# Key-value sums in the ring of PSUM banks, later query and rounding work, and both scan patterns in one PSUM bank, in a fused attention, expert and feed-forward kernel

## The chip, the cores and the metric

The kernel runs on one core of one Trainium2 chip. The metric is the device time of one execution in microseconds (us), the median of the runs shown.

The names in what follows: TensorE does matmuls and transposes, VectorE, ScalarE and GpSimd work on elements, and SyncE (SP) issues DMAs. They take their instructions in program order, each its own, and wait for one another by semaphores. SBUF is the on-chip memory of 128 partitions. PSUM, into which TensorE writes, is divided into banks of 512 fp32 columns per partition.

## The reference

Three layers in a row: a gated linear attention over 4 batches, 8 heads, 768 positions and 48 channels; a mixture of 8 experts with capacity 384 for 3072 tokens of width 384; and a dense feed-forward layer of width 2048.

```python
def _attn_ref(q, k, v, f_logit):
    f = 1.0 / (1.0 + np.exp(-f_logit))
    state = np.zeros((B, H, D, D))
    for t in range(S):
        state = f[:, :, t, :, None] * state + einsum('bhd,bhe->bhde', k[:, :, t], v[:, :, t])
        y[:, :, t] = einsum('bhd,bhde->bhe', q[:, :, t], state)
...
def _moe_ref(x, w_gate, w1, w2):          # N, D, E, F = 3072, 384, 8, 1024; cap = N // E
    order = np.argsort(-(x @ w_gate).flatten())
    # greedily: a token takes its best expert that has room
    for e in range(E):
        h = np.maximum(x[assigned == e] @ w1[e], 0.0)
        out[assigned == e] = h @ w2[e]
...
def _moe2_ref(x, w_in, w_out):            # d_ff 2048
    h = x @ w_in
    g = h * np.clip(h + 3.0, 0.0, 6.0) / 6.0
    return g @ w_out
```

The two weights of the last layer, w_in (384x2048) and w_out (2048x384), come as 64-bit floats.

## The kernel before

**Stages.** Attention takes about the first 175 us of the execution. Routing (which token goes to which expert) follows to about 200 us, and then the experts and the feed-forward layer, one expert at a time, to the end. The order of the instructions on each engine is that in which the Python code calls them (a schedule written out by hand); a waiting instruction holds back all that stand behind it on its engine.

**Attention by chunks.** 3072 tokens are 24 chunks (j) of 128, two of them a unit (u) of 256; there are 12 units, and 3 units are a batch. The recurrence is turned into matmuls inside a chunk and a state of 48x48 per head that goes from chunk to chunk. For this the queries are multiplied by the product of the decays from the chunk's start (the prefix scan, L97), the keys by the product from their place to the chunk's end divided by the whole (the suffix scan, L105). Each scan runs over 260 columns on VectorE, two heads' pairs (p) and both chunks (c) at once, and h=0 and h=1 name its two halves of the four pairs. `tensor_tensor_scan` goes along the columns, multiplies what it has by the decay and takes the maximum with a second tensor, the pattern. The prefix pattern m0 has a 1 where a chunk starts (the scan starts anew there) and 0 elsewhere. The suffix pattern m1 has the reciprocal of the chunk's whole product at its end. `ends` makes it: it takes the maximum of the prefix scan's last column and the limit PMIN (2^-60) into `pmin` (L100) and the reciprocal of that (L101).

**Banks.** m0, the key-value sums KV (L212 writes them) and the limit share one PSUM bank, pC, held for the whole stage; m1 is a pair of SBUF tiles. The other results of TensorE go through a ring of five banks, pT, or through pA0 and pA1 (the masked score products).

**One step of the loop** (lines 269 to 303) handles chunk j and prepares a later unit in eight slots, four in the step of an odd chunk and four in the next step, of an even one (`tg`, PET for TensorE, OPS for VectorE). In the order of the code: slots 0 and 1; the state matmuls of chunk j (L150, from state St) between score matmuls of chunk j+1 (L144, `ya_mm`); the copy of the scores by ScalarE and the causal mask by GpSimd (L177); the output matmuls (L201); the key-value matmuls (L212, `kv_mm`); a query part; slot 2; a decay or query part; the transpose of the keys (`kt_mm`) with ScalarE's copy kt; slot 3. `kv_mm` puts the state's update into the list `late`, which the next slot works off: VectorE adds the sums to the state (L219), GpSimd multiplies by `pmin` (L220). `logits` (L228) goes through the same list.

**refill** prepares a unit's inputs in parts: f by ScalarE and VectorE (L75 to L77), k by VectorE and ScalarE (L80, L81), q by GpSimd (L84 multiplies the even rows, L85 copies the odd ones). After the last part it issues the load of the next unit's input.

**Side work.** `prep` is a generator that VectorE works off in steps beside the attention. `prep_in` (lines 925 to 938) joins the two 32-bit words of each weight of w_in into an fp32 number, 12 tiles of 128x512 from the buffers pw (two, filled by a DMA each): L920, L922 and L924, one step each. Behind L924 it issues the fetch for the tile after the next (into the buffer now free), and splits the number: ScalarE rounds it to fp32r (wih, L717), GpSimd subtracts (wil, L718). `prep_out` (lines 940 to 957) does the like for w_out, in tiles of 128x384; its rounding (L955) is on ScalarE and its subtraction (L957) on VectorE, one step later. How many steps a slot takes is set by two tables:

```python
        PREP=((2,0,1,0),(0,1,1,0)); END=(1,0)
```

The first four numbers are those of the four slots in the step of an odd chunk, the second those of an even one, and END has the two at the step's end. Within a slot the steps come after the slot's first VectorE operation, and before the rest and the late list. The second half of w_out's 16 groups is left for the routing stage (GAP) and the first expert (O1).

Of the kernel before, what the change touches and what calls it, by code (L numbers as in the profile page):

```python
# [17 lines left out]
def attention(tc, q,k,v,f,wg, x_dram, lg, ident, pmin, ranges, prep, setup, spin):  # L18
    nc=tc.nc
    ctx=ExitStack()  # L20
    with ctx:
# [13 lines left out]
        held=ps.tile([128,512],F32,name="pC"); m0=held[:,:W2]; KV=held[:,W2:W2+NP*D].rearrange("p (a d) -> p a d",a=NP)  # L35
        nc.vector.memset(held[:,:W2],0.0); nc.vector.memset(held[:,W2+NP*D:],PMIN)
        nc.vector.memset(m0.rearrange("p (c t) -> p c t",t=L)[:,:,0:1],1.0)
        least=held[:,W2+NP*D:W2+NP*D+1,None].to_broadcast([128,2,2])
        m1=[]
        for i in range(2):  # L40
            t=cs.tile([128,W2],F32,name=f"m1{i}"); nc.vector.memset(t,0.0); m1.append(t)
# [40 lines left out]
        def queries(u,i,h0=0,h1=H):  # L82
            x=view(u,'q')[:,:,h0:h1]
            if i==0: nc.gpsimd.tensor_tensor(out=home('q',0)[:,h0:h1],in0=x[:,0],in1=ft[:,0,h0:h1],op=OP.mult)  # L84
            else: nc.gpsimd.tensor_scalar(home('q',1)[:,h0:h1],x[:,1],1.0,0.0,op0=OP.mult,op1=OP.add)  # L85
        KH={};QT={};PC={};PX={};SX={}
        V=nc.vector
        def decays(u,pairs):
            pt=ps.tile([128,512],F32,name="pT",bufs=PB).rearrange("p (a c g) -> p a c g",a=NP,c=2)
            for p in pairs: nc.tensor.transpose(pt[:,p].rearrange("p c g -> p (c g)"),perm['f'][:,p].rearrange("p a d -> p (a d)"),ident)  # L90
            for h in sorted({p//2 for p in pairs}):
                ff=FF[h][:,:W2].rearrange("p (a c g) -> p a c g",a=2,c=2)
                nc.scalar.copy(ff[:,:,:,1:],pt[:,2*h:2*h+2])
        def prefix(u,h):
            PX[u,h]=wk.tile([128,2,2,L],F32,name="P",bufs=2)
            x=PX[u,h]
            V.tensor_tensor_scan(x.rearrange("p a c g -> p (a c g)"),FF[h][:,:W2],m0,1.0,op0=OP.mult,op1=OP.max)  # L97
        def ends(u,h):
            PC[u]=pmin[:,u]; c=PC[u][:,2*h:2*h+2]
            V.tensor_tensor(out=c,in0=PX[u,h][:,:,:,G],in1=least,op=OP.max)  # L100
            V.reciprocal(m1[h].rearrange("p (a c g) -> p a c g",a=2,c=2)[:,:,:,G],c)  # L101
        def suffix(u,h):
            SX[u,h]=wk.tile([128,2,2,L],F32,name="S",bufs=2)
            x=SX[u,h].rearrange("p a c g -> p (a c g)")
            V.tensor_tensor_scan(x[:,::-1],FF[h][:,1:W2+1][:,::-1],m1[h][:,::-1],0.0,op0=OP.mult,op1=OP.max)  # L105
# [7 lines left out]
        def scaled(u,nm,h):  # L113
# [4 lines left out]
            x=(SX if nm=='k' else PX)[u,h]  # L118
# [8 lines left out]
        OPS={1:((prefix,0),(ends,0)),2:((prefix,1),(suffix,0)),3:((scaled,'q',0),(ends,1)),4:((scaled,'k',0),(suffix,1)),5:((scaled,'q',1),),7:((scaled,'k',1),)}  # L127
# [77 lines left out]
        def kv_mm(j):  # L205
# [3 lines left out]
            pk=KV  # L209
# [35 lines left out]
        for h in range(2):  # L245
# [9 lines left out]
            warm(WARM[1+h])  # L255
        for nm in 'fqk': load(1,nm)
# [11 lines left out]
        PREP=((2,0,1,0),(0,1,1,0)); END=(1,0)  # L268
        for j in range(-1,NCH+1):
# [20 lines left out]
            if ti==1: refill(tu+1,'q',0)  # L290
            tg(2)
            if ti==0: refill(tu+1,'f',0)
            if ti==1: refill(tu+1,'q',1)
            if j+1<NCH: kt_mm(j+1)
            tg(3)
# [610 lines left out]
def gla_moe_ffn(tc,q,k,v,f_logit,moe_w_gate,moe_w1,moe_w2,moe2_w_in,moe2_w_out,out):  # L906
    nc=tc.nc
    with ExitStack() as ctx:
# [16 lines left out]
        def prep_in(pool):  # L925
# [6 lines left out]
            yield  # L932
            for i in range(12):
                yield
                m=pool.tile([128,512],F32,name="pm",bufs=2); c=slice(i%4*512,i%4*512+512)
                yield from join(m,got[i])
                fetch(i+2)
                split_raw(nc,m,wih[:,i//4,c],wil[:,i//4,c],nc.gpsimd)
        woh={}; wol={}
        def prep_out(pool,wr,g0,g1,ahead,W=DM):  # L940
# [7 lines left out]
            for g in range(g0,g1):  # L948
                yield
                m=pool.tile([128,W],F32,name="pm",bufs=2)[:,:DM]  # L950
                yield from join(m,words[g])
# [3 lines left out]
                nc.scalar.copy(woh[g],m)  # L955
                yield
                nc.vector.tensor_tensor(out=wol[g],in0=m,in1=woh[g].bitcast(F32),op=OP.subtract)  # L957
# [177 lines left out]
```

## Time and profile before

| | |
|---|---|
| median of 3 runs (lowest to highest) | 853.25 us (848.27 to 855.46) |
| the profiled execution | 849.52 us |
| its span in the trace | 847.6 us |
| TensorE busy | 795.2 us (94%) |
| VectorE busy | 556.5 us (66%) |
| ScalarE busy | 358.2 us (42%) |
| GpSimd busy | 144.2 us (17%) |
| mean granted TensorE clock | 0.982 |

The span reaches from the first to the last instruction of the trace, and times within it are counted from its start. Busy is the time in which an engine has an instruction at work; TensorE's matmuls are pipelined, so a busy TensorE is not one at its peak. The shares are means over stages with different limits. The granted clock is the share of TensorE's full clock of 2.4 GHz that it got; 0.5 is its lower level, 1.2 GHz. Line numbers (L97) are those of the kernel before; those of the changed kernel lie a few further on (its L98 is L97 before).

### The profile page before, as it was taken

The page shows a single profiled execution, that of the slowest core. Times are in us where ns is not written, and L with a number is a line of the kernel's source. Part 1 is how long each engine was busy: PE and PEld are TensorE (multiplying, and loading weights), DVE is VectorE, ACT ScalarE, POOL GpSimd, SP SyncE. Part 2 cuts the span into 40 slices and gives each one's busy share as a digit, 9 for nine tenths or more (in the row PEclk, how much of TensorE's full clock was granted, in tenths as well). Part 3 has the DMA queues.
Part 4 walks back from the last instruction along what each step waited for, and adds up shares of the span by engine and source line. Part 5 has one row for each costly group of instructions (what it writes and reads, how often), then busy time and mean ns, then how long its engine had stood idle before and what let it go on. Part 6 is the DMA issues. An engine that isn't in the chain of part 4 may idle for free.

```text
span 847.6 us, 16704 instructions
## 1 busy us (share of the span) xinstructions
PE 795.2 (94%) x6387; PEld 763.4 (90%) x6387; DVE 556.5 (66%) x1541; ACT 358.2 (42%) x732; POOL 144.2 (17%) x228
## 2 busy tenths in 40 slices
PE   7788798888999999999999999999999999999994
PEld 6677687778999899999999999999999999999994
DVE  7879899767679647845975676667766523642431
ACT  4656566415244415422542354155315423641431
POOL 3655755202001100110101101100200020010001
PEclk9989999987999999999999999999999999999998
DMA  9877798155004202311421232222232331321000
GB/s 224 204 203 192 205 255 216 50 193 163 1 1 122 84 17 78 91 50 56 122 81 60 83 111 81 88 87 86 79 99 72 97 94 56 113 84 47 10 1 32
DMA packets 99033, 84.55 MB, mean 100 GB/s; under 512 B 67328, under 2 KB 86912, under 8 KB 98944
## 3 DMA queue, kind: packets, MB, share of 16 engines
q1 hardware_dynamic: 95872, 73.96, 31.2%
q0 software_dynamic: 3072, 9.44, 3.5%
q8 instruction: 52, 0.85, 0.4%
q14 instruction: 37, 0.30, 0.1%
HBM read 73.94 MB, written 9.44 MB: 98 GB/s over the span
## 4 chain that ended last, share of the span: by engine, by line
PE 56%; issue 10%; DVE 8%; ACT 3%; DMA 1%; POOL 1%; POOLq 0%; DVEq 0%; ACTq 0%; SPq 0%
PE pF L721 9%; PE acc L721 9%; PE pF L722 9%; PE pF L723 9%; PE acc L723 9%; PE acc L722 9%; DVE ga L864 2%; DVE hl L867 1%; ACT hh L866 1%; ACT ga L863 1%; DVE w1l L770 1%; PE pF L808 1%; POOL out_dram L898 1%; DMA wst<-in_moe_w_dram 1%; DVE q_ge L499 0%
## 5 line engine op out<-in xcount | busy, mean ns | idle before, releaser
L721 PE MATMUL acc<-wo,hh 128*128 128x384 f32 x384 | 133.6, 348 | 0.0
L864 DVE SCALAR_TENSOR_TENSOR ga<-ga,pF 128x384 f32<-128x384 f32 x128 | 70.7, 553 | 92.5 <-ACT ga L863 92.0
L721 PE MATMUL pF<-xh,wih 128*128 128x384 f32 x384 | 131.0, 341 | 0.0
L722 PE MATMUL pF<-xh,wil 128*128 128x384 f32 x384 | 129.4, 337 | 0.0
L723 PE MATMUL acc<-wo,hh 128*128 128x384 f32 x384 | 129.3, 337 | 0.0
L723 PE MATMUL pF<-xl,wih 128*128 128x384 f32 x384 | 129.3, 337 | 0.0
L722 PE MATMUL acc<-wo,hl 128*128 128x384 f32 x384 | 129.1, 336 | 0.1
L863 ACT ACTIVATE ga<-pF,three 128x384 f32<-128x384 f32 x128 | 74.2, 579 | 96.7 <-PE pF L723 89.7
L866 ACT CAST hh<-ga 128x384 fp32r<-128x384 f32 x128 | 65.8, 514 | 97.4 <-DVE ga L864 92.6
L898 POOL DMA_INDIRECT out_dram<-ga,q_ids x24 | 24.3, 1011 | 395.7 <-ACT ga L896 393.0
L867 DVE TENSOR_TENSOR hl<-ga,hh 128x384 fp32r<-128x384 f32 x128 | 71.1, 556 | 29.7 <-ACT hh L866 27.7
L829 ACT ACTIVATE hh<-pF 128x384 fp32r<-128x384 f32 x64 | 31.5, 492 | 132.1 <-PE pF L723 123.1
L830 DVE SCALAR_TENSOR_TENSOR hl<-pF,hh 128x384 fp32r<-128x384 f32 x64 | 35.5, 555 | 70.8 <-ACT hh L829 70.5
L721 PEld LDWEIGHTS acc<-wo,hh 128*128 128x128 f32 x384 | 72.2, 188 | 1.6 <-ACT ga L863 1.5
L722 PEld LDWEIGHTS acc<-wo,hl 128*128 128x128 f32 x384 | 72.2, 188 | 0.4 <-DVE hl L867 0.4
L722 PEld LDWEIGHTS pF<-xh,wil 128*128 128x128 f32 x384 | 72.2, 188 | 0.0
L721 PEld LDWEIGHTS pF<-xh,wih 128*128 128x128 f32 x384 | 72.2, 188 | 0.0
L723 PEld LDWEIGHTS pF<-xl,wih 128*128 128x128 f32 x384 | 72.1, 188 | 0.0
L723 PEld LDWEIGHTS acc<-wo,hh 128*128 128x128 f32 x384 | 72.0, 188 | 0.0
L721 PE MATMUL pF<-xh,w1h 128*128 128x384 f32 x192 | 67.1, 350 | 0.6 <-ACT xh L799 0.6
L721 PE MATMUL acc<-hh,w2h 128*128 128x384 f32 x192 | 65.9, 343 | 0.0
L722 PE MATMUL pF<-xh,w1l 128*128 128x384 f32 x192 | 65.2, 340 | 0.0
(284 smaller groups left out, 1636.7 us busy)
## 6 DMA issues: line engine op xcount, KB each, us to landing
wst<-in_moe_w_dram SPq DMA_DIRECT2D x58, 192.0 KB, 2.4
wst<-in_moe_w_dram SPq DMA_DIRECT2D x42, 256.0 KB, 2.8
pw<-in_moe_w_in_dram SPq DMA_DIRECT2D x12, 512.0 KB, 4.4
wo<-in_moe_w_out_dram SPq DMA_DIRECT2D x16, 384.0 KB, 5.2
pm<-in_moe_w_out_dram SPq DMA_DIRECT2D x32, 192.0 KB, 2.4
pm<-in_moe_w_in_dram SPq DMA_DIRECT2D x30, 192.0 KB, 2.5
v<-in_v_dram SPq DMA_DIRECT2D x24, 192.0 KB, 4.8
x_dram<-y SPq DMA_DIRECT2D x24, 192.0 KB, 5.0
```

Of the source, the lines that this page charges most:

```text
L721: nc.tensor.matmul(out, ahi, bhi, start=start, stop=False)
L722: nc.tensor.matmul(out, alo, bhi, start=False, stop=False)
L723: nc.tensor.matmul(out, ahi, blo, start=False, stop=stop)
L770: nc.vector.tensor_tensor(out=lo,in0=got[i],in1=hi.bitcast(F32),op=OP.subtract)
L808: nc.tensor.transpose(p[:,h*128:(h+1)*128],s.xg[:,h,d*128:(d+1)*128],s.ident)
L829: nc.scalar.activation(hh,p,AF.Relu)
L830: s.defer(2,lambda: nc.vector.scalar_tensor_tensor(hl,p,0.0,hh.bitcast(F32),op0=OP.max,op1=OP.subtract))
L863: nc.scalar.activation(a,p,AF.Relu,bias=s.three[:,0:1])
L864: late(f,1,lambda: nc.vector.scalar_tensor_tensor(g,a,6.0,p,op0=OP.min,op1=OP.mult))
L866: late(f,1,lambda: nc.scalar.copy(gh,g))
L867: late(f,3,lambda: nc.vector.tensor_tensor(out=gl,in0=g,in1=gh.bitcast(F32),op=OP.subtract))
L898: st=nc.gpsimd.indirect_dma_start(out=s.out,out_offset=bass.IndirectOffsetOnAxis(ap=ids[:,t:t+1],axis=0),in_=o,in_offset=None)
```

## The change

1. m0 gets the limit: at the column ahead of each chunk's start, which is the chunk's last product, the pattern holds PMIN, so that the prefix scan itself takes the maximum there. L100 goes, the reciprocal reads the scan's output, and `pmin` is written by a new small ScalarE copy per unit (`kept`), behind slot 2 in the steps of odd chunks. The scans run over 259 columns instead of 260. P becomes two tiles that stay, one per unit in turn.
2. m1 is one pattern instead of two, in the same PSUM bank as m0, and its reciprocal for h=1 stands in slot 2 behind the suffix scan of h=0.
3. KV goes into the ring pT, which stays at five banks.
4. The parts of q come behind `kt_mm`, and ScalarE copies the odd rows.
5. `prep_in` splits a tile one step later than it joins it; `prep_out` rounds a group in the first step of the next group, and subtracts between that one's first and second join. PREP and END change.

```diff
-        held=ps.tile([128,512],F32,name="pC"); m0=held[:,:W2]; KV=held[:,W2:W2+NP*D].rearrange("p (a d) -> p a d",a=NP)
-        nc.vector.memset(held[:,:W2],0.0); nc.vector.memset(held[:,W2+NP*D:],PMIN)
-        nc.vector.memset(m0.rearrange("p (c t) -> p c t",t=L)[:,:,0:1],1.0)
-        least=held[:,W2+NP*D:W2+NP*D+1,None].to_broadcast([128,2,2])
-        m1=[]
+        held=ps.tile([128,512],F32,name="pC"); m0=held[:,:W2-1]; m1=held[:,512-W2:]
+        nc.vector.memset(held,0.0)
+        for n in range(4):
+            nc.vector.memset(held[:,n*L+G-1:n*L+G],PMIN)
+            if n: nc.vector.memset(held[:,n*L-1:n*L],1.0)
+        PXB=[]
         for i in range(2):
-            t=cs.tile([128,W2],F32,name=f"m1{i}"); nc.vector.memset(t,0.0); m1.append(t)
+            t=cs.tile([128,NP,2,L],F32,name=f"P{i}"); nc.vector.memset(t,1.0); PXB.append(t)
...
-            else: nc.gpsimd.tensor_scalar(home('q',1)[:,h0:h1],x[:,1],1.0,0.0,op0=OP.mult,op1=OP.add)
+            else: nc.scalar.copy(home('q',1)[:,h0:h1],x[:,1])
...
         def prefix(u,h):
-            PX[u,h]=wk.tile([128,2,2,L],F32,name="P",bufs=2)
-            x=PX[u,h]
-            V.tensor_tensor_scan(x.rearrange("p a c g -> p (a c g)"),FF[h][:,:W2],m0,1.0,op0=OP.mult,op1=OP.max)
+            PX[u]=PXB[u%2]
+            V.tensor_tensor_scan(flat(PX[u][:,2*h:2*h+2])[:,1:],FF[h][:,1:W2],m0,1.0,op0=OP.mult,op1=OP.max)
         def ends(u,h):
-            PC[u]=pmin[:,u]; c=PC[u][:,2*h:2*h+2]
-            V.tensor_tensor(out=c,in0=PX[u,h][:,:,:,G],in1=least,op=OP.max)
-            V.reciprocal(m1[h].rearrange("p (a c g) -> p a c g",a=2,c=2)[:,:,:,G],c)
+            V.reciprocal(m1.rearrange("p (a c g) -> p a c g",a=2,c=2)[:,:,:,G],PX[u][:,2*h:2*h+2,:,G])
+        def kept(u):
+            PC[u]=pmin[:,u]
+            nc.scalar.copy(PC[u],PX[u][:,:,:,G])
...
-            V.tensor_tensor_scan(x[:,::-1],FF[h][:,1:W2+1][:,::-1],m1[h][:,::-1],0.0,op0=OP.mult,op1=OP.max)
+            V.tensor_tensor_scan(flat(SX[u,h])[:,1:][:,::-1],FF[h][:,2:W2+1][:,::-1],m1[:,1:][:,::-1],0.0,op0=OP.mult,op1=OP.max)
...
-        OPS={1:((prefix,0),(ends,0)),2:((prefix,1),(suffix,0)),3:((scaled,'q',0),(ends,1)),4:((scaled,'k',0),(suffix,1)),5:((scaled,'q',1),),7:((scaled,'k',1),)}
+        OPS={1:((prefix,0),(ends,0)),2:((prefix,1),(suffix,0),(ends,1)),3:((scaled,'q',0),),4:((scaled,'k',0),(suffix,1)),5:((scaled,'q',1),),7:((scaled,'k',1),)}
...
-            pk=KV
+            pk=ps.tile([128,512],F32,name="pT",bufs=PB)[:,:NP*D].rearrange("p (a d) -> p a d",a=NP)
...
-        PREP=((2,0,1,0),(0,1,1,0)); END=(1,0)
+        PREP=((2,0,1,0),(0,0,2,0)); END=(0,1)
...
             if j>=0: kv_mm(j)
-            if ti==1: refill(tu+1,'q',0)
             tg(2)
+            if ti==0 and tu<NU: kept(tu)
             if ti==0: refill(tu+1,'f',0)
-            if ti==1: refill(tu+1,'q',1)
             if j+1<NCH: kt_mm(j+1)
+            if ti==1:
+                for i in range(2): refill(tu+1,'q',i)
             tg(3)
...
+            split=lambda: None
             for i in range(12):
                 yield
+                split()
                 m=pool.tile([128,512],F32,name="pm",bufs=2); c=slice(i%4*512,i%4*512+512)
                 yield from join(m,got[i])
                 fetch(i+2)
-                split_raw(nc,m,wih[:,i//4,c],wil[:,i//4,c],nc.gpsimd)
+                split=lambda i=i,m=m,c=c: split_raw(nc,m,wih[:,i//4,c],wil[:,i//4,c],nc.gpsimd)
+            yield
+            split()
...
-            for g in range(g0,g1):
+            done=None
+            for g in range(g0,g1+1):
                 yield
-                m=pool.tile([128,W],F32,name="pm",bufs=2)[:,:DM]
-                yield from join(m,words[g])
+                if done: nc.scalar.copy(woh[g-1],done)
+                if g<g1:
+                    m=pool.tile([128,W],F32,name="pm",bufs=2)[:,:DM]
+                    parts=join(m,words[g]); next(parts)
+                yield
+                if done: nc.vector.tensor_tensor(out=wol[g-1],in0=done,in1=woh[g-1].bitcast(F32),op=OP.subtract)
+                if g==g1: return
+                yield
+                next(parts)
+                yield
+                next(parts,None)
                 fetch(g+ahead)
                 w=wr.tile([128,2,DM],F32R,name=f"wo{g}")
                 woh[g],wol[g]=w[:,0],w[:,1]
-                nc.scalar.copy(woh[g],m)
-                yield
-                nc.vector.tensor_tensor(out=wol[g],in0=m,in1=woh[g].bitcast(F32),op=OP.subtract)
+                done=m
```

GpSimd's program in one unit of the attention stage, first before and then in the change. am is the masked score, pmq the query, St the state, wil the subtraction's result; r_ones and r_zero are constants of the routing.

```order
L718 TENSOR_TENSOR wil<-pm,wih 128x512
L177 AFFINE_SELECT am<-am 128x512 x2
L84 TENSOR_TENSOR pmq<-qr,ft 128x8x48
L220 TENSOR_TENSOR St_124<-St_122,pmin 128x4x48
L85 TENSOR_SCALAR pmq<-qr 128x8x48
L390 MEMSET r_ones 128x128
L391 MEMSET r_zero 128x24
L718 TENSOR_TENSOR wil<-pm,wih 128x512
L177 AFFINE_SELECT am<-am 128x512 x2
L220 TENSOR_TENSOR St_122<-St_124,pmin 128x4x48
```

```order
L178 AFFINE_SELECT am<-am 128x512 x2
L221 TENSOR_TENSOR St_129<-St_127,pmin 128x4x48
L721 TENSOR_TENSOR wil<-pm,wih 128x512
L85 TENSOR_TENSOR pmq<-qr,ft 128x8x48
L393 MEMSET r_ones 128x128
L394 MEMSET r_zero 128x24
L721 TENSOR_TENSOR wil<-pm,wih 128x512
L178 AFFINE_SELECT am<-am 128x512 x2
L221 TENSOR_TENSOR St_127<-St_129,pmin 128x4x48
```

In the first half of what is shown (an even chunk), the subtraction wil stood ahead of the masks and the query product between masks and state; in the change both stand behind the state multiply, and the query's copy (L85 before) is gone from this engine. In the second half the order is as it was.

VectorE's program from one state sum to the next and on to the next unit's first scan, before. qt and kh are the scaled queries and keys, S the suffix scan's and P the prefix scan's output, m its pattern, pm and pw the joined tile and its words, lg the logits, pmf and pmk the decays and the keys; scans are printed as SCALAR_TENSOR_TENSOR.

```order
L219 TENSOR_TENSOR St_124<-St_124,pC 128x4x48
L124 TENSOR_TENSOR qt<-pT,P 128x512
L100 TENSOR_TENSOR pmin<-P,pC 128x4
L101 RECIPROCAL m_108<-pmin 128x4
L922 SCALAR_TENSOR_TENSOR pm<-pw,pm 128x512
L124 TENSOR_TENSOR kh_121<-pT,S 128x512
L105 SCALAR_TENSOR_TENSOR S<-ff_128,m_108 128x260
L124 TENSOR_TENSOR qt<-pT,P 128x512
L924 SCALAR_TENSOR_TENSOR pm<-pw,pm 128x512
L228 TENSOR_REDUCE lg<-pT 128x8
L77 TENSOR_TENSOR pmf<-ft 128x8x48
L219 TENSOR_TENSOR St_122<-St_122,pC 128x4x48
```

The same stretch in the change:

```order
L220 TENSOR_TENSOR St_129<-St_129,pT 128x4x48
L125 TENSOR_TENSOR qt<-pT,P_113 128x512
L125 TENSOR_TENSOR kh_126<-pT,S 128x512
L106 SCALAR_TENSOR_TENSOR S<-ff_133,pC 128x259
L125 TENSOR_TENSOR qt<-pT,P_113 128x512
L229 TENSOR_REDUCE lg<-pT 128x8
L78 TENSOR_TENSOR pmf<-ft 128x8x48
L220 TENSOR_TENSOR St_127<-St_127,pT 128x4x48
```

Between the two sums the maximum L100, the reciprocal and the two join steps are gone; the rest stands as it stood.

VectorE's program behind that second sum up to the next unit's first scan, before:

```order
L920 TENSOR_SCALAR pm<-pw 128x512
L124 TENSOR_TENSOR kh_121<-pT,S 128x512
L80 TENSOR_TENSOR pmk<-kr,ft 128x8x48
L922 SCALAR_TENSOR_TENSOR pm<-pw,pm 128x512
L924 SCALAR_TENSOR_TENSOR pm<-pw,pm 128x512
L97 SCALAR_TENSOR_TENSOR P<-ff_126,pC 128x260
```

And in the change:

```order
L927 SCALAR_TENSOR_TENSOR pm<-pw,pm 128x512
L923 TENSOR_SCALAR pm<-pw 128x512
L125 TENSOR_TENSOR kh_126<-pT,S 128x512
L81 TENSOR_TENSOR pmk<-kr,ft 128x8x48
L925 SCALAR_TENSOR_TENSOR pm<-pw,pm 128x512
L927 SCALAR_TENSOR_TENSOR pm<-pw,pm 128x512
L923 TENSOR_SCALAR pm<-pw 128x512
L98 SCALAR_TENSOR_TENSOR P_111<-ff_131,pC 128x259
```

Where three join steps stood, five stand: a tile's last step (L927), all three of another tile, and the first (L923) of a third one, which uses the buffer that the first L927 read.

## Rows read from the trace of the kernel before

**Rows 1.** Windows: start:end, length; busy us per engine; PE clock; DMA share; GB/s.

```profile
27.43:150.92 123.49, 101.58 (x1724) 91.14 (x1721) 108.93 (x223) 76.57 (x166) 73.64 (x116) 0.97 0.83 210
40.23:56.70 16.47, 12.60 (x200) 11.27 (x200) 11.57 (x25) 8.36 (x18) 9.29 (x15) 0.90 0.74 192
87.08:101.47 14.39, 11.12 (x212) 9.92 (x206) 12.49 (x25) 8.36 (x18) 10.84 (x17) 1.00 0.83 211
```

The engines stand in the order PE, PEld (weight loads), DVE (VectorE), ACT (ScalarE), POOL (GpSimd); the number of instructions is in parentheses.

**Rows 2.** Waits of VectorE, 27.43 to 150.92: us in total, times, longest.

```profile
DVE P L97 <- PE pC L212: 8.5, 6, 4.7
DVE qt L124 <- PE pT L111: 2.2, 1, 2.2
DVE wo L957 <- ACT wo L955: 1.2, 2, 0.6
DVE St L219 <- PE pC L212: 0.8, 2, 0.4
DVE St L217 <- PE pC L212: 0.3, 1, 0.3
```

**Rows 3.** Timeline of VectorE: start, us, instruction, [idle before, and its releaser].

```profile
82.01 0.35 DVE L219 TENSOR_TENSOR St<-St,pC 128x192 f32<-128x192 f32 x1 [0.40 <-PE pC L212]
...
84.77 1.48 DVE L922 SCALAR_TENSOR_TENSOR pm<-pw,pm 128x512 uint32<-128x512 uint32 x1
...
89.73 0.70 DVE L97 TENSOR_TENSOR_SCAN P<-ff,pC 128x260 f32<-128x260 f32 x1 [1.32 <-PE pC L212]
...
91.27 0.33 DVE L219 TENSOR_TENSOR St<-St,pC 128x192 f32<-128x192 f32 x1
...
92.40 0.66 DVE L922 SCALAR_TENSOR_TENSOR pm<-pw,pm 128x512 uint32<-128x512 uint32 x1
...
96.41 0.35 DVE L219 TENSOR_TENSOR St<-St,pC 128x192 f32<-128x192 f32 x1 [0.40 <-PE pC L212]
...
101.47 0.68 DVE L97 TENSOR_TENSOR_SCAN P<-ff,pC 128x260 f32<-128x260 f32 x1
```

**Rows 4.** Timeline of GpSimd in the same unit.

```profile
83.01 1.42 POOL L177 TENSOR_SCALAR_AFFINE_SELECT am<-am 128x512 f32<-128x512 f32 x2
84.40 1.29 POOL L84 TENSOR_TENSOR pmq<-qr,ft 128x384 f32<-128x384 f32 x1
85.66 0.95 POOL L220 TENSOR_TENSOR St<-St,pmin 128x192 f32<-128x192 f32 x1
```

**Rows 5.** Timeline of TensorE in two units, from state matmul to key-value matmul.

```profile
41.69 0.48 PE L150 MATMUL pT<-qt,St 64*64 64x128 f32 x2 [3.08 <-POOL St L220]
...
45.60 0.62 PE L212 MATMUL pC<-v,kt 128*64 128x48 f32 x16
...
86.67 0.33 PE L150 MATMUL pT<-qt,St 64*64 64x128 f32 x2 [2.44 <-POOL St L220]
...
89.06 0.62 PE L212 MATMUL pC<-v,kt 128*64 128x48 f32 x16
```

**Rows 6.** Windows, as rows 1, of two microseconds behind the first.

```profile
42.00:44.00 2.00, 2.00 (x44) 2.00 (x40) 0.00 (x0) 0.00 (x0) 1.57 (x4) 0.50 0.72 243
```

**Rows 7.** Groups by form, 30 to 166: times, busy us, mean ns, idle before.

```profile
L105 DVE TENSOR_TENSOR_SCAN S<-ff,m 128x260 f32<-128x260 f32 x20 | 16.8, 839 | 0.0
L97 DVE TENSOR_TENSOR_SCAN P<-ff,pC 128x260 f32<-128x260 f32 x18 | 12.4, 688 | 8.6 <-PE pC L212 8.6
...
L81 ACT COPY pmk<-kr 128x384 f32<-128x384 f32 x9 | 4.9, 540 | 0.0
L100 DVE TENSOR_TENSOR pmin<-P,pC 128x4 f32<-128x4 f32 x19 | 2.9, 154 | 0.3
```

**Rows 8.** DMA issues on the page: times, KB each, median us to landing.

```profile
pw<-in_moe_w_in_dram SPq DMA_DIRECT2D x12, 512.0 KB, 4.4
```

**Rows 9.** Waits of VectorE, 150.92 to 166.

```profile
DVE wo L957 <- ACT wo L955: 2.3, 4, 0.6
DVE P L97 <- PE pC L212: 0.5, 1, 0.5
```

More of the change, by code (lines that the diff above doesn't have):

```diff
@@ L93, in decays @@
                 nc.scalar.copy(ff[:,:,:,1:],pt[:,2*h:2*h+2])
+        flat=lambda t: t.rearrange("p a c g -> p (a c g)")
         def prefix(u,h):
-            PX[u,h]=wk.tile([128,2,2,L],F32,name="P",bufs=2)
-            x=PX[u,h]
-            V.tensor_tensor_scan(x.rearrange("p a c g -> p (a c g)"),FF[h][:,:W2],m0,1.0,op0=OP.mult,op1=OP.max)
+            PX[u]=PXB[u%2]
+            V.tensor_tensor_scan(flat(PX[u][:,2*h:2*h+2])[:,1:],FF[h][:,1:W2],m0,1.0,op0=OP.mult,op1=OP.max)
         def ends(u,h):
-            PC[u]=pmin[:,u]; c=PC[u][:,2*h:2*h+2]
-            V.tensor_tensor(out=c,in0=PX[u,h][:,:,:,G],in1=least,op=OP.max)
-            V.reciprocal(m1[h].rearrange("p (a c g) -> p a c g",a=2,c=2)[:,:,:,G],c)
+            V.reciprocal(m1.rearrange("p (a c g) -> p a c g",a=2,c=2)[:,:,:,G],PX[u][:,2*h:2*h+2,:,G])
+        def kept(u):
+            PC[u]=pmin[:,u]
+            nc.scalar.copy(PC[u],PX[u][:,:,:,G])
         def suffix(u,h):
             SX[u,h]=wk.tile([128,2,2,L],F32,name="S",bufs=2)
-            x=SX[u,h].rearrange("p a c g -> p (a c g)")
-            V.tensor_tensor_scan(x[:,::-1],FF[h][:,1:W2+1][:,::-1],m1[h][:,::-1],0.0,op0=OP.mult,op1=OP.max)
+            V.tensor_tensor_scan(flat(SX[u,h])[:,1:][:,::-1],FF[h][:,2:W2+1][:,::-1],m1[:,1:][:,::-1],0.0,op0=OP.mult,op1=OP.max)
         PT={}
@@ L117, in scaled @@
             pt=PT.pop((u,nm,h))
-            x=(SX if nm=='k' else PX)[u,h]
+            x=SX[u,h] if nm=='k' else PX[u][:,2*h:2*h+2]
             x=x.rearrange("p a c g -> p (a c) g")
@@ L255, in attention @@
             warm(WARM[1+h])
+        kept(0)
         for nm in 'fqk': load(1,nm)
```

## The prediction

> **What bounds the kernel now.** The mean rows by stage come first. From 201 us on TensorE streams matmuls and the change touches little there; the change lies in the attention stage, 0 to about 175 us, so I cut that stage by its own clock, the unit (one h=0 scan L97 to the next). Nine units, 27.43 to 150.92, take 123.49 us, 13.72 each [rows 1]. VectorE is busy 108.93 us of them, TensorE 101.58, ScalarE 76.57, GpSimd 73.64, and the DMA engines at a share of 0.83. So VectorE sets the pace, with 14.56 us of idle time, and TensorE is close behind: a unit can fall only until one of the two, or the state chain that runs through both, is full.
>
> The view of waits says what the idle time is. The second scan of a unit (L97) waits 8.5 us in six places for the key-value matmul L212, up to 4.7 us [rows 2]. That scan reads nothing of L212; both only use bank pC. A query product waits 2.2 us and state sums 0.8 and 0.3 for matmuls of TensorE, and L957 waits 1.2 us in two places, 0.6 each, for the rounding ScalarE has just been given. Together that is 13.0 us.
>
> The timelines of one unit, 87.08 to 101.47, show why L212 is late. The state sum of the chunk before ends on VectorE at 82.36, but GpSimd multiplies it only at 85.66, behind two mask selects (83.01) and the query product L84 (84.40) [rows 3, 4]. TensorE waits 2.44 us for it and starts its state matmuls at 86.67; the key-value matmuls run from 89.06 to 89.68, and the scan starts at 89.73, 1.32 us late [rows 3, 5]. In the unit from 40.23 the same wait was 3.08 us; after it TensorE's granted clock was 0.50, its lower level, and the way from state matmul to key-value matmul took 41.69 to 45.60, 3.9 us where the later unit needs 2.4 [rows 5, 6]. That unit took 16.47 us with VectorE busy 11.57 [rows 1].
>
> **The change part by part**, for the nine units first.
>
> *Limit in the scan.* Two L100 go per unit, at 154 ns [rows 7]: 18 x 0.154 = **-2.8 us**. Their outputs now come from one small ScalarE copy per unit, which waits for the second scan; ScalarE is 62% busy, and I cost it at nothing. If its cover were gone it would hold back the kt copy behind it, and with it the logit matmuls, by a few tenths per unit: it is in the upper bound.
>
> *Suffix scan reads pC instead of m1.* The suffix scan L105 takes 839 ns on average and the prefix scan L97, which reads the bank already, 688 [rows 7]. That work of VectorE on SBUF is stretched beside GpSimd, the join step L922 shows: 1.48 us at 84.77, beside the query product, and 0.66 at 92.40 [rows 3, 4]. I take the whole difference, 18 x 0.151 = **-2.7 us**; bounds 0 (GpSimd's work stretches a neighbour instead) and 2.7. The Trainium skill (SBUF — State Buffer, Who interferes with whom) says that a VectorE instruction with two SBUF inputs contends with a GpSimd instruction that reads SBUF, and one with at most one does not; by that rule the stretch of L105 goes entirely, and the rows agree with it.
>
> *kv in the ring, q and wil behind the state.* The second scan then waits for no matmul, and GpSimd's order puts the state multiply right behind the selects, ahead of wil and L84 (the order rows on GpSimd). In the unit above it could start near 84.4 instead of 85.66, or sooner, since wil no longer stands ahead of the selects; the matmuls of that half move forward by 1.3 to 2.4 us, which ends VectorE's 1.32 us wait and leaves the 4.7 us one no cause. Of the 14.56 us idle I drop the 13.0 of the waits above: 8.5 for L97, 2.2, 0.8 and 0.3 that followed the same late matmuls, 1.2 for L957: **-13.0 us**. The order of work bounds it: 14.56 at most, and little at the least (third rival).
>
> *What is late next: the state chain.* In the order rows on VectorE, L922 and L924 stood between the two state sums of a unit; in the change their like stand outside. The chain from one sum to the next is unchanged: sum at 91.27, state matmul 1.11 us later, and from state matmul to the point where VectorE can go on 89.73 - 86.67 = 3.06 [rows 3, 5]: 4.17 us. The work that VectorE now has in between is 96.01 - 91.27 = 4.74 (to 96.41 less 0.40, where the next sum began to wait) less an L100 (and part of L101), 0.3, less L922 and L924, at about 0.6 each: 3.2 us. So the second sum waits about 0.9 us in each of the six of the nine units that carry the state in both halves: **+5.4 us**; bounds 2.4 (0.40 each, as the wait before the sum at 96.41 is now [rows 3]) and 8.5 (the ring's new kt release adds half a microsecond).
>
> *The pw fetch.* By the order rows, tile B's last join step L927 now stands with five instructions between it and the next use of its buffer (L923). The fetch for that use is issued by the end of L927. Five instructions of the same kinds ran from the sum's end at 96.76 to 101.47, 4.71 us [rows 3]; a fetch lands 4.4 us after issue [rows 8], and for issue and semaphore I allow 0.5. That is 0.2 us late. If GpSimd stretched fewer of the five (L922's 0.66 for its 1.48) they would take some 2 us less. I take 0.5 us in five units: **+2.5 us**, bounds 0 and 10.
>
> *Outside the nine units.* Behind 150.92 go one L97 wait of 0.5 and three of the four L957 waits of 0.6 (the last lies where VectorE no longer sets the pace) [rows 9]: **-2.2 us**, bounds 0.8 and 3.5, the more if the masks no longer queue behind a rounding. In routing L957 stands on the path with such a wait too, and with the roundings a step later that goes and one join step leaves the gap before: **-1.0 us**, by one wait of 0.6 and two thirds of an L922 (0 to 1.3). At the start VectorE sets seven single columns (at most an L100 each, 1.1) and clears two tiles of twice the size (at most an L922 each, 1.3), while the first loads are under way: **+0.5 us**, bounds 0 and 2.4.
>
> *At nothing:* the query copy, now 0.54 us of ScalarE per unit [rows 7] instead of GpSimd work; it stands behind a rounding and the kt copy and ahead of the decay copies that the next h=0 scan needs. That scan comes over 4 us later on VectorE (96.76 to 101.47 [rows 3]), against some 3 us of copies; without that cover it costs 0.5 per unit.
>
> Sum: -2.8 - 2.7 - 13.0 + 5.4 + 2.5 - 2.2 - 1.0 + 0.5 = **-13.3 us**. The profiled execution took 849.52 us, so 836.2; it lies 3.7 below the median of the three runs shown, 853.25, and the same step from there gives 840. I forecast **838 us**. The nine units come to about 113 us, 12.5 each.
>
> **Rivals.** (1) *The clock falls in the new wait.* TensorE will idle about 1.9 us per unit ahead of the second half's state matmuls, for the sum that VectorE reaches late. For it: 3.08 us of idle was followed by 0.50. Against: 2.44 was not (clock 1.00 from 87.08 on) [rows 1, 5, 6]. Price: 3.9 - 2.4 = 1.5 us, on the chain each time, six units: +9, so 847. The Trainium skill (TensorE: Matmul & The Clock Gate, HAM oscillation — how this bites in real kernels) warns that a wait repeated in every turn of a loop can throttle every turn anew; by that rule it would be every unit, and the trace shows it in the longer waits only.
>
> (2) *DMA takes the gain.* The nine units hold 0.83 x 123.49 = 102.5 us of DMA time; in 113 us that is a share of 0.91. If transfers start to wait, and the units stay at 0.85, they take 120.6: +7.7, so 846. Against: of VectorE's waits in these units none is for a transfer [rows 2].
>
> (3) *The change doesn't do what it says.* If the state multiply stays as late (its sum is late on VectorE rather than queued on GpSimd), the wait only moves from the scan to the state sum, and the -13.0 and +5.4 fall away: -5.7, so 844.
>
> (4) *The other side: the pw fetch is late.* Six times in the stage VectorE would stand at L923 with the scan, and so the whole unit, behind it. The gain is gone when each stall is 0.5 + 13.3 / 6 = 2.7 us, at a landing of about 7 us; at 9 us it is 4.7 each, +25 on the sum, so 861. Against: 4.4 us is the landing now, with the queries and keys not yet issued at that moment.
>
> (5) *More than forecast:* neither new wait appears: 828.
>
> **How the numbers follow.** Forecast (831 to 843) 0.53; rival 1 0.08, 2 0.12, 3 0.13, 4 0.07, rival 5 0.07. The forecast's own range is 831 to 843; the range to 8 in 10 reaches down to rival 5 and up past 1 and 2: 828 to 848. About 1% (8.5 us against 853.25, so 844.7) is what a measurement of this kernel can tell from no change. Faster: forecast, rival 5 and most of rival 3, 0.70; same: 1, 2 and the rest of 3, 0.23; slower: 4, 0.07.
>
> **What would show it.** Right: no L97 wait for a matmul; L105's heir at 0.69 in every place; GpSimd's state multiply within 0.1 us of its sum in second halves; waits of 0.4 to 1.4 us before the second sum of a unit; units near 12.5 us and a granted clock of 1.00 throughout. Wrong: clock rows of 0.50 between 40 and 110 (rival 1), VectorE waiting for pw by microseconds (4) or for k (2), the state multiply still microseconds behind its sum (3). The forecast as a whole is wrong if the nine units take over 120 us.

## The result, and the profile after

| | before | changed |
|---|---|---|
| median (lowest to highest) | 853.10 us (848.27 to 855.46) | 843.22 us (839.63 to 845.23) |
| ratio, 95% interval | | 0.9882, 0.9855 to 0.9909 |
| the profiled execution, its span | 849.52, 847.6 us | 845.23, 843.2 us |
| nine units (first scan to first scan) | 123.49 us | 117.97 us |
| VectorE busy, idle in them | 108.93, 14.56 us | 101.42, 16.55 us |
| mean granted clock | 0.982 | 0.982 |

The change made the kernel faster by 9.9 us or 1.2%: the side that was forecast, at two thirds of the size (838 us). The median of 843.22 lies 0.2 us above the forecast's own range (831 to 843) and inside the wide one (828 to 848). The two profiled executions differ by only 4.3 us, since the one of before was among its fastest and the one of after is its slowest; sums over the two traces therefore fall 5.6 us short of the medians.

The windows of after, columns as in [rows 1], give all nine units, a usual one, a long one, and six microseconds within the long one:

```profile
27.78:145.75 117.97, 101.63 (x1724) 91.14 (x1722) 101.42 (x203) 80.58 (x183) 65.97 (x107) 0.97 0.87 220
41.71:55.59 13.88, 11.10 (x188) 9.78 (x188) 12.13 (x24) 9.00 (x22) 9.07 (x14) 1.00 0.84 221
82.60:99.36 16.76, 14.20 (x188) 12.64 (x188) 12.07 (x23) 8.91 (x21) 9.23 (x14) 0.80 0.78 183
86.28:92.28 6.00, 6.00 (x68) 5.49 (x70) 2.72 (x6) 2.39 (x5) 1.89 (x6) 0.50 1.22 249
```

VectorE's work fell by 7.5 us (the maxima L100 are gone, the suffix scans take 12.3 us instead of 15.4, and one join step and one subtraction fewer fall into the stretch), but its idle time did not fall, it rose. What it waits for is another thing now. The view of waits of VectorE over the nine units, which answers to [rows 2]:

```profile
DVE St L220 <- PE pT L213: 9.7, 6, 4.1
DVE pm L923 <- DMA wo<-in_moe_w_out_dram: 2.5, 1, 2.5
DVE pm L923 <- DMA pw<-in_moe_w_in_dram: 2.1, 3, 1.0
DVE lg L229 <- ACT y L232: 0.5, 1, 0.5
```

The second scan waits for nothing any more. Instead the second state sum of a unit (L220, L219 before) waits for the key-value matmul, six times, and the join waits for its words. GpSimd does what it was to do: the state multiply that belongs to the second sum of a unit now follows the masks, ahead of the subtraction and the query product. It starts 0.1 us behind its sum in all six places, where it was 0.6 to 4.8 us behind before, 3.3 us in the unit shown there [rows 3, 4]. One second sum of after on VectorE, then GpSimd:

```profile
76.83 0.35 DVE L220 TENSOR_TENSOR St<-St,pT 128x192 f32<-128x192 f32 x1 [1.12 <-PE pT L213]
```

```profile
75.96 1.22 POOL L178 TENSOR_SCALAR_AFFINE_SELECT am<-am 128x512 f32<-128x512 f32 x2 [2.08 <-ACT am L177]
77.27 0.89 POOL L221 TENSOR_TENSOR St<-St,pmin 128x192 f32<-128x192 f32 x1
78.52 1.28 POOL L721 TENSOR_TENSOR wil<-pm,wih 128x512 fp32r<-128x512 f32 x1 [0.36 <-ACT wih L720]
79.76 1.32 POOL L85 TENSOR_TENSOR pmq<-qr,ft 128x384 f32<-128x384 f32 x1
```

### The profile page after: what moved, and what is told of

Its sections match the earlier page's. It is cut to its first block, busy times and chain, and to the rows that moved or that the text cites. A ratio compares the mean times of both kernels' runs of the same rounds, so it can differ in the third digit from the quotient of the medians.

```text
span 843.2 us, 16692 instructions
## 1 busy us (share of the span) xinstructions
PE 793.5 (94%) x6387; PEld 761.9 (90%) x6387; DVE 549.6 (65%) x1522; ACT 364.0 (43%) x757; POOL 134.7 (16%) x215
## 4 chain that ended last, share of the span: by engine, by line
PE 57%; issue 10%; DVE 8%; ACT 2%; DMA 2%; POOL 1%; POOLq 0%; SPq 0%; DVEq 0%; ACTq 0%
PE pF L724 9%; PE acc L724 9%; PE pF L725 9%; PE pF L726 9%; PE acc L726 9%; PE acc L725 9%; DMA xg<-x_dram,q_ids 1%; DVE ga L867 1%; DVE hl L870 1%; ACT hh L869 1%; DVE w1l L773 1%; PE pF L811 1%; POOL out_dram L901 1%; DVE q_ge L502 1%; POOL xg L790 1%
## 5 line engine op out<-in xcount | busy, mean ns | idle before, releaser
L726 PE MATMUL pF<-xl,w1h 128*128 128x384 f32 x192 | 64.9, 338 | 0.0
```

What stands on the lines that cost most here:

```text
L726: nc.tensor.matmul(out, ahi, blo, start=False, stop=stop)
```

## The experiments

All medians are of executions timed beside the kernel before on the same chip (its median 851.9 us in the first four runs, 852.7 in the next four, 851.1 in the last four).

| run | what it is | median (lowest to highest) | ratio to before, 95% interval |
|---|---|---|---|
| e1 | before, key-value sums in the ring | 847.10 (845.1 to 850.3) | 0.9942 (0.9919 to 0.9965) |
| e2 | changed, key-value sums back | 845.12 (844.13 to 846.62) | 0.9918 (0.9891 to 0.9946) |
| e3 | changed, suffix pattern back in SBUF | 843.24 (841.58 to 845.57) | 0.9905 (0.9875 to 0.9935) |
| e4 | changed, order of side work back | 842.84 (839.00 to 846.34) | 0.9904 (0.9873 to 0.9936) |
| e5 | changed, handling of joined tiles back | 836.94 (835.06 to 838.31) | 0.9820 (0.9792 to 0.9848) |
| i1 | changed, split at the step's end | 843.48 (840.88 to 843.86) | 0.9891 (0.9866 to 0.9915) |
| i2 | changed, three word buffers | 842.01 (840.24 to 842.89) | 0.9877 (0.9853 to 0.9901) |
| i4 | i1 with the old tables | 835.05 (833.72 to 837.26) | 0.9806 (0.9778 to 0.9834) |
| e7 | changed, old tables: two join steps between the sums | 835.95 (834.92 to 836.66) | 0.9821 (0.9796 to 0.9846) |
| e8 | changed, one join step between | 834.43 (833.49 to 838.80) | 0.9814 (0.9785 to 0.9842) |
| e9 | changed, none between, the others spread | 840.48 (836.83 to 842.02) | 0.9864 (0.9839 to 0.9890) |
| i5 | i4 with w_out's first fetches earlier | 835.59 (833.81 to 837.32) | 0.9818 (0.9793 to 0.9843) |

### e1: the ring alone

```diff
-            pk=KV
+            pk=ps.tile([128,512],F32,name="pT",bufs=PB)[:,:NP*D].rearrange("p (a d) -> p a d",a=NP)
```

> The kernel before with one part of the change alone: the key-value sums go into the ring of five banks instead of pC. Theory (the prediction's): the second scan then waits for no matmul, which takes the 9.0 us of its waits away; the state multiply on GpSimd stays behind the query product, so TensorE still waits some 14 us for it, and the sums that VectorE then reaches sooner wait a little longer. Expected 844 to 848 us against 853, second-scan waits 0, waits of the state sums 3 to 5 us in place of 0.8. Rival A (the wait only moves from the scan to the state sum): 850 to 854, with state-sum waits of 8 us or more. Rival B (the ring of five banks gets too small with one user more): 853 or slower, with TensorE waiting for ScalarE's copies out of the ring by 10 us or more.

Measured 847.1, in the theory's range. VectorE's waits show that both it and rival A had a part: no scan waits, but the state sums wait 6.9 us in place of 0.8, near A's 8.

```profile
DVE St L219 <- PE pT L212: 6.9, 6, 3.3
DVE qt L124 <- PE pT L111: 3.3, 3, 1.7
```

So of 9.0 us of scan waits some 5 were gained. Rival B falls: no wait of TensorE for a copy of yt passes 0.8 us.

### e2: the ring undone in the changed kernel

KV goes back to `held[:,W2:W2+NP*D]` and L214 writes there; the suffix pattern goes to SBUF, as in e3.

> The changed kernel with the key-value sums back in bank pC; as they don't fit beside both patterns, the suffix pattern is back in two SBUF tiles. The limit in the scan and the new order stay. Theory: the second scan waits again for the key-value matmul of the step, some 5 to 9 us, and the suffix scans cost 2.7 us more: 849 to 853 against 843 of the change. Rival A (the ring only moves the wait): 844 to 847, the suffix scan's 2.7 alone, with state-sum waits small again. Rival B (the ring is too small in the change): 841 to 844, and TensorE's waits for the copies of yt, 13.7 us in the change, mostly gone.

Measured 845.1, the time of rival A, though not by its reason, as the state sums still wait. With this order the scan comes late, and the shared bank couples the other way: now the matmul waits for the scan more than the scan for the matmul. Waits of VectorE, then of TensorE, over its nine units:

```profile
DVE St L221 <- PE pC L214: 6.3, 6, 1.9
DVE P L99 <- PE pC L214: 3.9, 6, 1.0
```

```profile
PE pC L214 <- DVE P L99: 8.9, 5, 3.7
```

### e3: the suffix pattern in SBUF

```diff
-held=ps.tile([128,512],F32,name="pC"); m0=held[:,:W2-1]; m1=held[:,512-W2:]
+held=ps.tile([128,512],F32,name="pC"); m0=held[:,:W2-1]
...
+            t=cs.tile([128,W2],F32,name=f"m1{i}"); nc.vector.memset(t,0.0); m1.append(t)
```

> The changed kernel with the suffix pattern alone back in two SBUF tiles; the key-value sums stay in the ring. Theory: the suffix scans are stretched beside GpSimd again, mean 0.83 us instead of 0.68 in 20 of them: 845 to 847 against 843. Rival (the stretch only moves to the VectorE instruction beside it, or into waits that are there anyway): 842 to 844, though the suffix scan's mean goes up.

The rival's result: 843.24 against 843.22, though the scan's mean went from 682 to 832 ns. The groups by form over nine units, first of after, then of e3:

```profile
L106 DVE TENSOR_TENSOR_SCAN S<-ff,pC 128x259 f32<-128x259 f32 x18 | 12.3, 682 | 0.0
```

```profile
L107 DVE TENSOR_TENSOR_SCAN S<-ff,m 128x259 f32<-128x259 f32 x18 | 15.0, 832 | 0.0
```

The 2.7 us are there in the scan and not in the time. In after VectorE is busy 101.42 us and idle 16.55 in the nine units, in e3 103.30 and 12.78: what the scan saves became waiting. One of a unit's two suffix scans lies between the state sums, where VectorE waits anyway; that this hides it is argued, no run isolates it.

e2 and e3 differ in the ring alone, 845.12 and 843.24 us. So with the new order the ring is worth 1.9 us by the medians, and the executions of the two overlap, where it gave 4.8 by itself (e1).

### e4: the old order of the side work

The query parts, the split, `prep_out` and the tables are those of before; the ring and both patterns stay.

> The changed kernel with its order of side work undone: the query parts ahead of the transposes and on GpSimd as before, the split of a joined tile right behind the join, the old tables of steps. The ring and the two patterns in one bank stay. Theory: the state multiply stands behind the query product again, so TensorE waits for it again (7 to 14 us in place of 0.2), of which VectorE's state sums show some; the waits for the fetched words (4.6 us) go: 845 to 849 against 843. Rival C (the new order gives nothing, since ScalarE's rounding now stands ahead of the copies of the next step and waits for the join, 19 us, and TensorE waits 13.7 us for the copies of yt behind it): 839 to 844.

Measured 842.84, the same as the change: rival C's time. TensorE waits for the state multiply again, 10.7 us:

```profile
PE pT L151 <- POOL St L221: 10.7, 6, 2.4
```

So the whole new order is worth nothing. Either its parts do nothing or one takes what another gives. Rival C named a taker: ScalarE's rounding. The next four runs take the parts one by one.

### e5, i1, i2 and i4: which part takes it

e5 has `prep_in`, `prep_out` and the tables of before. i2 has `bufs=3` for pw and fetches three tiles ahead. i1 collects the splits in a list and works it off at the end of the loop's step; i4 is i1 with the old tables.

```diff
-                split=lambda i=i,m=m,c=c: split_raw(nc,m,wih[:,i//4,c],wil[:,i//4,c],nc.gpsimd)
+                SPLITS.append(lambda i=i,m=m,c=c: split_raw(nc,m,wih[:,i//4,c],wil[:,i//4,c],nc.gpsimd))
...
+            while SPLITS: SPLITS.pop(0)()
             if j>=0: next(constants,None)
```

> The changed kernel with only its handling of the joined tiles undone (split right behind the join, old tables of steps); q stays late and partly on ScalarE, the ring and the patterns stay. Theory H (in the change ScalarE's rounding, now beside the next tile's first join step, stands ahead of the copies of the next step and waits up to 2.6 us for the join's last step on VectorE; TensorE waits 13.5 us for the copies of yt behind it, and this eats what the late q gives): 837 to 841 against 843, with TensorE's waits for yt below 4 us and those for the state multiply below 8 us. Rival F (it is the late fetches, 4.6 us of VectorE's waits): these go here too, 838 to 841, but TensorE's waits for yt stay. Rival N (neither was on the path, since another chain has the same length): 842 to 845.

> The changed kernel with the split of a joined tile (ScalarE's rounding and GpSimd's subtraction) issued at the end of the loop's step, behind the query and key copies, when the join's last step is long done. Nothing else moves. Theory H: ScalarE's waits for the join, 19.1 us in the change, fall below 6; TensorE's waits for yt fall from 13.5 to below 4; 838 to 841 against 843. Rival F: the late fetches stay (4.6 us), 842 to 844. Rival N: 842 to 845, and the waits turn up elsewhere.

> The changed kernel with three buffers for the fetched words instead of two, each fetch a tile earlier; nothing else moves. Rival F (late fetches are what the change pays with): VectorE's waits for pw, 2.1 us, go, and 840 to 842 against 843. Theory H: the rounding's wait on ScalarE and TensorE's wait for yt stay as they are, and VectorE only waits for its state sums instead: 842 to 844.

> As the run with the split at the end of the loop's step, and with the old tables of steps too, so that two join steps stand between the state sums again and the fetches are spread more evenly. Theory H with F: no wait for pw, none of ScalarE for the join, none of TensorE for the state multiply or yt: 836 to 840. By the prediction's fourth step (the state chain is next once VectorE has less work between the sums) this is 1 to 3 us faster than with the new tables; rival (that chain does not bind): the same within 1 us.

e5 took 836.9 us, 6 less than the change and than e4: the late query is worth that much, and the handling of the joined tiles, tables included, takes it. Theory H (the rounding) falls by i1: TensorE's waits for yt, 13.5 us, fell to 1.6, and the time stayed at 843.5. ScalarE only waits elsewhere; its waits in after, then in i1:

```profile
ACT wih L720 <- DVE pm L927: 19.1, 12, 2.6
```

```profile
ACT pmin L104 <- DVE P L99: 16.0, 7, 4.2
```

Both are waits for VectorE, which is the engine that is late. Rival F (the words) falls as the main cause by i2: no wait for pw is left, and the median is 1.2 us lower, within the uncertainty. i4 differs from i1 in the tables alone and took 835.05 against 843.48 on the same chip; their executions don't overlap. The tables cost 8.4 us (7 by the ratios).

### e7, e8, e9 and i5: what about the tables

```diff
-        PREP=((2,0,1,0),(0,0,2,0)); END=(0,1)
+        PREP=((2,0,1,0),(0,1,1,0)); END=(1,0)
```

```diff
-        PREP=((2,0,1,0),(0,0,2,0)); END=(0,1)
+        PREP=((2,0,1,0),(0,1,2,0)); END=(0,0)
```

```diff
-        PREP=((2,0,1,0),(0,0,2,0)); END=(0,1)
+        PREP=((1,0,3,0),(0,0,2,0)); END=(0,0)
```

These are e7, e8 and e9. Between the second sum of a unit and the first of the next stand six join steps in after and e9, five in e8 and four in e7. i5 draws the start of `prep_out`, with its first three fetches, ahead of the 31st step of `prep_in`.

> The changed kernel with only the two tables of steps back, so that two join steps stand between the two state sums of a unit again (none in the change) and three in a row ahead of the next unit's first scan (five in the change). The split stays a step late. Theory C (the chain from state sum to state sum through TensorE is longer than the work that the new tables leave VectorE between the sums, so VectorE waits and TensorE after it): state-sum waits fall from 12.2 us in eight to under 5; 835 to 838 against 843. Theory P (the five join steps in a row hold up the next unit's scans, and with them TensorE): the same time, since both are undone. Theory H (the split's place is what costs): 841 to 844.

> The changed kernel with tables that put one join step between the two state sums and four ahead of the next first scan, two of them ahead of the keys' product. Theory C: about half the way, 838 to 841; state-sum waits 5 to 9 us. Theory P: 840 to 842, since the pile is one step shorter.

> The changed kernel with tables that leave no join step between the state sums, as the change does, but spread the others: three ahead of the next first scan instead of five, three behind the unit's second scan. Theory C: 842 to 845, state-sum waits of 10 us or more. Theory P: 836 to 839, though no step stands between the sums.

e7, the tables alone undone, took 835.95; e8, with one join step between the sums, 834.43, all of the gain and not half of it; e9, with none between, 840.48. By theory C e9 should have been at 842 or more, by P at 839 or less; it lies between. By the medians most of the price is that of the empty place between the sums. That the pile of five has a share is not shown: the executions of e9 and of the change overlap, and e9 has no wait for fetched words in the nine units, of which after has 4.6 us (two kinds, w_in's and w_out's). e7 beside e5 (835.95 and 836.94, ratios 0.9821 and 0.9820) says one thing more: with the old tables, it makes no difference whether the split stands right behind the join or a step later.

The timelines of VectorE, state sums only, first two units of after, then one unit and the next first sum of e8 and of e7:

```profile
30.82 0.34 DVE L220 TENSOR_TENSOR St<-St,pT 128x192 f32<-128x192 f32 x1
...
35.42 0.36 DVE L220 TENSOR_TENSOR St<-St,pT 128x192 f32<-128x192 f32 x1 [1.32 <-PE pT L213]
...
44.80 0.34 DVE L220 TENSOR_TENSOR St<-St,pT 128x192 f32<-128x192 f32 x1
...
49.07 0.36 DVE L220 TENSOR_TENSOR St<-St,pT 128x192 f32<-128x192 f32 x1 [0.99 <-PE pT L213]
```

```profile
31.15 0.34 DVE L220 TENSOR_TENSOR St<-St,pT 128x192 f32<-128x192 f32 x1
...
35.75 0.35 DVE L220 TENSOR_TENSOR St<-St,pT 128x192 f32<-128x192 f32 x1 [0.72 <-PE pT L213]
...
43.61 0.34 DVE L220 TENSOR_TENSOR St<-St,pT 128x192 f32<-128x192 f32 x1
```

```profile
30.32 0.34 DVE L220 TENSOR_TENSOR St<-St,pT 128x192 f32<-128x192 f32 x1
...
35.06 0.34 DVE L220 TENSOR_TENSOR St<-St,pT 128x192 f32<-128x192 f32 x1
...
43.42 0.34 DVE L220 TENSOR_TENSOR St<-St,pT 128x192 f32<-128x192 f32 x1
```

From the first sum of a unit to the second it takes 4.60 us in after and in e8, where VectorE waits for the second sum, and 4.74 in e7, where it doesn't. So the chain through GpSimd and TensorE sets it in the first two (4.27 to 4.60 us in the full-clock units of after), and one join step there is free. From the second sum to the next first one it takes 9.38, 7.86 and 8.36 us. There VectorE waits for nothing but words (0.43 us in after), so its own work sets the time, but not by the count of steps: e7 has one step fewer there than e8 and takes 0.5 us longer, since its key product and its join steps take longer beside GpSimd. The key products, first e7, then e8:

```profile
36.44 1.50 DVE L81 TENSOR_TENSOR pmk<-kr,ft 128x384 f32<-128x384 f32 x1
```

```profile
37.88 1.03 DVE L81 TENSOR_TENSOR pmk<-kr,ft 128x384 f32<-128x384 f32 x1
```

One unit took 13.88 us in after (41.71 to 55.59) and 12.47 in e8 (40.60 to 53.07):

```profile
40.60:53.07 12.47, 11.72 (x202) 10.18 (x199) 11.65 (x24) 8.64 (x21) 9.04 (x13) 1.00 0.96 242
```

The 1.41 us are 0.27 of the sum's wait (0.99 to 0.72), 0.65 of a wait for pw that e8 hasn't in this unit, and 0.48 of VectorE's busy time (12.13 to 11.65), the join steps and the key product being stretched more in after. Such a wait for pw stands in three of the nine units of after.

The clock seems to have a share too. e9 and e8 differ by 6.1 us over the nine units of their traces, and all of it lies in the two units of e9 in which the granted clock fell; the other seven take 83.6 us in e9 and 83.8 in e8 (which waits 3.1 us for words there). Not all of it need be the clock's, as VectorE is also busy 1.9 us longer in the first of the two. The two units of e9, then the same two of e8:

```profile
27.33:43.75 16.42, 14.14 (x240) 13.00 (x231) 13.50 (x24) 10.25 (x23) 8.99 (x14) 0.90 0.76 188
68.74:83.53 14.79, 12.66 (x196) 11.43 (x198) 11.91 (x24) 9.39 (x22) 8.70 (x14) 0.88 0.85 216
```

```profile
28.15:40.60 12.45, 12.09 (x226) 10.96 (x224) 11.63 (x24) 9.25 (x22) 9.08 (x13) 1.00 1.00 244
66.60:78.97 12.37, 10.60 (x196) 9.71 (x196) 11.55 (x24) 7.40 (x18) 7.12 (x12) 1.00 0.94 236
```

At full clock the four other units with both sums took 49.4 us in e9 and 47.1 in e8, so by these two traces the empty place costs 0.6 us in each, on average. Of the 9.3 us between after and e8, 4.3 lie in the one unit of after whose clock fell; of the 8.0 between i1 and i4, 5.2 lie in two such units of i1.

> The run with the split at the step's end and the old tables, which took 835.05 us, with the first three fetches of w_out's words issued some two tiles earlier. There VectorE waited 3.2 us for the first of them, once. If that wait is on the path: 831 to 833, and no wait of L925 for w_out left. If the wait only stands where VectorE would wait for the state anyway: 834 to 836.

i5 took 835.59, the second case: no wait for w_out was left, but VectorE's busy time in the nine units went from 103.27 to 106.08 us, and one unit had a granted clock of 0.84.

The best of these runs, e8, is 0.9814 of before, 16.7 us; it cannot be told from i4, e7, i5 and e5.

## Why the prediction was right, and where it was off

**The sign was right, the size was 5 us too large, at the upper edge of the range.** The nine units were to take about 113 us and took 117.97. The work of VectorE fell by more than was said (7.5 us for 5.5); the miss is in its idle time, which was to fall by 5.1 us and rose by 2.0. Of these 7.1 us, 4.3 are the waits of the state sums (9.7 for 5.4, above the bound of 8.5) and 2.5 a wait for w_out's words. Step by step:

*The cause, the late state multiply and the shared bank:* right. No scan waits for a matmul, and TensorE's wait for the multiply fell from 13.8 us in seven places to 0.2 in one. The ring alone gave 4.8 us (e1), the late query about 6 (e4 to e5). Together with the other parts, but with the tables left as they were (e7), the gain is 15.2 us, where the prediction's terms without the two new waits come to 21.2. In the nine units of e7 VectorE's idle time fell from 14.56 to 3.73 us, so 10.8 of the 13.0 came; its work fell by 3.5 where 5.5 was said.

```profile
27.63:136.83 109.20, 98.42 (x1708) 87.75 (x1706) 105.47 (x202) 80.19 (x181) 67.25 (x107) 1.00 0.93 234
```

*Suffix pattern in PSUM, -2.7:* the scan does what was said, 682 ns everywhere, in agreement with the rule of the Trainium skill that the prediction named (SBUF — State Buffer, Who interferes with whom). The step that failed is to take the whole difference as a gain: the lower bound, 0, was right. In the change it made no difference (e3). Where VectorE hardly waits, in e7, the suffix scans' 15.4 us became 12.3, but the key product went from a mean of 919 ns to 1236 (2.8 us over nine), and the first join step from 648 to 778. Which part of the change put them beside GpSimd is open: between e3 and after, which differ in the pattern alone, the key product stays at 1020 ns.

*State chain, +5.4, and pw fetch, +2.5:* the mechanism and the place were right. The waits in full-clock units were 1.32, 0.99, 1.12, 0.92 and 1.31 us where 0.9 was said, since the chain took up to 4.60 us and not 4.17; one, in the unit whose clock fell, was 4.07. Undoing the tables, which removes both terms, gave 8.4 us (i4 against i1) where 7.9 was forecast; e7 against the change gives 7.3 by the medians and 5 by the ratios. That the whole comes so near may be luck in part, as these differences also hold the units whose clock fell. What the prediction lacked was the conclusion: it named this as a price and did not ask whether the step could be left out.

*A wait not foreseen:* the first fetch of w_out, 2.5 us, once. That the join had been moved nearer to it is not the whole cause, as e3 has the joins in the same order and no such wait. When it was taken away in i5, the time stayed as it was.

*Outside the units:* behind them the trace shows -1.5 (from 26.28 to 24.82 us up to the first routing step, 177.20 and 170.57), where -2.2 was said. Routing did not fall by 1.0 but took 24.78 us instead of 23.03 to the first expert matmul; TensorE waits 5.7 us there for gathered rows, 1.7 before. In before and the three runs with the old handling of the tiles (e1, e4, e5) this stretch took 22.4 to 23.8 us, in the change and the nine runs with the rounding moved 22.8 to 24.9, 1.1 us more on average. So the moved rounding may well cost here what it was to give; no run isolates it.

**The rivals.** Rival 1, the clock, came in one unit and not by the wait that it named: 0.50 from 86.28 on for six microseconds, 16.76 us where the four units ahead of it took 13.1 to 13.9, so some 3 us and not 9. The idle time ahead of it, 2.10 us, was for a copy of yt, ahead of the transposes; after has five such waits of 2.10 to 2.46 us in the nine units, and the clock fell behind one. The mean clock is that of before. Rival 2, DMA, falls: e8's nine units took 108.66 us at a DMA share of 0.94, above the 0.85 at which the rival held them; VectorE waits 3.1 us for words there all the same.

```profile
28.15:136.81 108.66, 97.98 (x1723) 88.09 (x1719) 100.30 (x203) 80.34 (x182) 67.58 (x107) 1.00 0.94 239
```

Rival 3 falls by the GpSimd rows above. Rival 4, the late words, came at 2.1 us in all, in three places, and not at 2.7 each.

**Left open:** how the 8.4 us of the tables divide into the sum's wait, the words, the stretch and the clock. In one unit the first three could be read off. The profiles of i4, e7 and e8 show none of the nine units below full clock, those of after, i1, i2 and e9 one or two at 0.78 to 0.90; but e5 (two units at 0.92 and 0.95) and i5 (one at 0.84) are as fast as the first. No run sets the clock by itself.

## What to carry to other kernels

Before work is moved out of the way of a chain, measure the chain from end to end (here 4.6 us from sum to sum, in the change and in e8): a join step within it was free, and the same step behind it lengthened the unit, by 0.6 us in e9 at full clock and by more in after. When a bundle of edits gives less than its parts promise, undo the parts one at a time; here one line of tables took back what the late query gave.

## What the runs showed of the hardware that was not expected

Which VectorE instructions are stretched beside GpSimd changes with the order of the steps alone. GpSimd's work is 66 to 68 us in the nine units of e7, e8 and after, but the key product, with two SBUF inputs, has a mean of 1236 ns in e7, 1020 in after and 924 in e8 (919 before). Freeing the scan (832 ns in e3, 682 in after) did not hand its stretch to others: the join steps and the key and decay products take 50.1 us together in e3 and 49.3 in after.

TensorE's clock fell to its lower level in after behind a wait of 2.10 us, and did not behind one of 2.46 us in a like place, nor behind one of 2.10 ahead of the same matmul (at 43.27). In e5 it was at 0.50 from 53 to 56 us, and the longest wait of TensorE in the 12 us before was 1.12. The timelines of TensorE in the two units; L227 takes 2.04 us at 0.50 and 1.04 at full clock:

```profile
56.92 0.66 PE L112 MATMUL pT<-ident,pmk 128*128 128x128 f32 x4 [2.46 <-ACT yt L203]
...
57.85 1.04 PE L227 MATMUL pT<-sw,yt 128*128 128x104 f32 x8
```

```profile
84.68 0.66 PE L185 MATMUL pT<-ident,kh 128*128 128x128 f32 x4 [2.10 <-ACT yt L203]
...
86.28 2.04 PE L227 MATMUL pT<-sw,yt 128*128 128x104 f32 x8
```

The wait of e5, and its clock:

```profile
52.26 0.33 PE L151 MATMUL pT<-qt,St 64*64 64x128 f32 x2 [1.12 <-POOL St L221]
```

```profile
53.00:56.00 3.00, 3.00 (x46) 2.67 (x42) 2.73 (x6) 1.81 (x4) 2.24 (x4) 0.50 0.70 187
```
